# Linear attention with a row norm and a gated feed-forward on one core: the start, the place of batch 2's loads, the norm chains, the query tails and the last tile are changed

## The chip, the core and the metric

The kernel runs on one core of a Trainium2 chip. The metric is device microseconds of one execution, as the median of three runs. A profile is one further execution of the same program, recorded by the hardware profiler. The core's engines are TensorE (PE, with weight loads shown as PEld), VectorE (DVE), ScalarE (ACT), GpSimd (POOL) and SyncE (SP), which here only issues DMAs. Each engine works through its own instructions in program order.

## The reference

For 8 batches and 8 heads, with 576 rows and 64 columns a head, without softmax:

```
kv  = k^T v                      per batch and head, 64 x 64
o   = q kv                       576 x 64
a   = o / sqrt(mean(o*o) + 1e-6) * g_norm          over the 64 columns
x   = a, heads side by side      4608 rows x 512
xn  = x / sqrt(mean(x*x) + 1e-6) * rms_g           over the 512 columns
g, val = xn @ w_gate, xn @ w_val                   512 x 1536 each
out = (g * sigmoid(g) * val) @ w_out               1536 x 512, result 4608 x 512 fp32
```

All inputs are fp32; the kernel rounds them to bf16 for the products.

## The kernel before

**Tiles.** Of each batch 512 rows are "main" (four tiles of 128, `T` = 4) and 64 are "tail". The tails of all eight batches are gathered into a ninth block, so that the feed-forward runs nine times over 512 rows: n = 0 to 7 for the batches, n = 8 for the tails. `Ffn.up(j)` makes 128 columns of gate and value (8 matmuls of 512 columns), `silu` on ACT, the product `h` on DVE; there are 12 of them. `Ffn.down(c)` multiplies `h` with w_out for one tile of 128 rows (12 matmuls), four times, and `down_out` copies the sum on ACT and stores it from SP.

**The order.** It is written out by hand; nothing is moved by a planner. While block n is in the feed-forward, the attention of n+1 is put between its steps by the lists `steps[u]` (u = 0 to 11 stand behind `up(u)`, 12 to 15 behind `down(u - 12)`): kv products, `o(c)` (PE, then a square and a copy on ACT), `sums(c)` (DVE), and at step 11 `chain` (DVE: both norms' factor alpha, with an inverse root by a bit trick and two Newton steps), `scale(c)` (DVE) and `x_rows(c)` (SP: a DMA transpose of a scaled tile into `xnt`, which the next block's `up(0)` reads).

**PSUM.** Four pools of two banks each: `gps` and `vps` for gate and value, `ops` for the output, `att` for attention. `up(j)` can start only when `silu` of `up(j-2)` has read its `gps` bank.

**Loads.** All loads but a few at the start go through SP, in program order, into the `stage` pool of seven buffers of 1 MB: batch 0, then the weights (`load_w`, four blocks), batch 1 and w_out (three blocks). Batch 2 is loaded in line 685, near the end of block 0, behind block 0's first store. `load_batch(n + 2)` at the start of block n does it for batch 3 and on. ACT casts batch 2's q in `steps[0]` and `steps[1]` of block 1, and `q_rows` (SP, DMA transposes, behind the loads of batch 3 on SP's queue) turns it for `o(0)` at step 6. For blocks 2 and on these casts and transposes are done one block earlier, behind the downs.

**Batch 0 and 1** use `Early`: the sums of squares are made on PE from a transposed output, `Early.chain` works on them in PSUM, and x is turned on PE (`turn`). For batch 0 this is the start of the kernel, with parts of `up` of 128 and 256 columns as soon as a tile of x is there. The sources are `first_kv`, `gammas`, lines 468 to 607.

**Query tails.** At the start of block 6 `load_q_tails` issues eight loads of 128 KB from SP; ACT casts them behind the downs of block 6 (`cast_q_tails`, two casts, one for the even and one for the odd batches) and SP turns them (`turn_q_tails`, eight DMA transposes) for the ninth block's `o(0)`, which stands at step 2 of block 7.

Of the kernel before, what the change touches and what calls it, by code (L numbers as in the profile page):

```python
# [1 line left out]

# [15 lines left out]
def kernel(  # L18
# [61 lines left out]
    mask = consts.tile([128, 128], FP32, name="mask")  # L80
    sqT = consts.tile([128, NS, MAIN], BF16, name="sqT")
# [95 lines left out]
    def chain(u, w, nc_, name):  # L177
# [10 lines left out]
        )  # L188
        yi = stat_pool.tile(shape, I32, name=name + "yi")
# [20 lines left out]
    class Att:  # L210
# [103 lines left out]
    class Ffn:  # L314
# [29 lines left out]
        def down_out(self, c):  # L344
            if c % 2 == 0:
                self.o_sb = osb_pool.tile([128, 2, d_model], FP32, name="o_sb")
            nc.scalar.copy(out=self.o_sb[:, c % 2, :], in_=self.o_ps[c])  # L347
            n = self.n
# [10 lines left out]
        def down(self, c):  # L359
            self.down_products(c, 0, NF)  # L360
# [21 lines left out]
    nc.scalar.preload_act_table(ACT.Silu)  # L382
# [11 lines left out]
    nc.vector.memset(warm_sb, 0.0)  # L394
    nc.vector.memset(sel, 0.0)
# [5 lines left out]
    nc.vector.memset(ones1, 1.0)  # L401
    nc.vector.memset(kv_all[:, 1:], 0.0)

    def warm(ps, count, w=256):
        for _ in range(count):
            nc.tensor.matmul(ps[:, 0:w], lhsT=identity, rhs=warm_sb[:, 0:w], start=True, stop=True)  # L406
# [4 lines left out]
    class Early:  # L411
# [62 lines left out]
    for half, engine in enumerate((nc.vector, nc.scalar)):  # L474
        ps = ops_pool.tile([128, 2, T, 128], BF16, name="o_ps")
        for j in range(2):
            for c in range(T):
# [4 lines left out]
                )  # L482
        cast(engine, first.qt[:, 2 * half : 2 * half + 2, :], ps.rearrange("p j c t -> p j (c t)"))
        if half == 0:
            cast_tail(0, "k", nc.vector)
            cast_tail(0, "v", nc.scalar)
            cast_piece(0, "k", 0, nc.vector)
            cast_piece(0, "v", 0, nc.scalar)
            cast_piece(0, "k", 1, nc.vector)

# [3 lines left out]

    def gammas():
        nc.vector.tensor_copy(out=gcol, in_=gam_ps[:, NS : NS + 1])
        nc.vector.tensor_scalar(
            out=rowscale, in0=gam_ps[:, 0:NS], scalar1=gcol[:, 0:1], scalar2=None, op0=OP.mult
        )
        for i in range(2):  # L500
            ps_ = slice(i * D, (i + 1) * D)
            nc.vector.scalar_tensor_tensor(
                out=sel[ps_, 1, i : i + 1], in0=gcol[ps_, :], scalar=1.0 / d_model, in1=gcol[ps_, :],
                op0=OP.mult, op1=OP.mult,
            )
# [4 lines left out]
    def first_kv(j):  # L510
        hs = slice(2 * j, 2 * j + 2)
        ps = att_pool.tile([128, 128], FP32, name="att_ps")
        warm(ps, 3, 128)
# [5 lines left out]

    cast_piece(0, "v", 1, nc.scalar)  # L520
    first_kv(0)
    gammas()
    first_kv(1)
    sq_ps = [first.out_turned(0, gps_pool, "g_ps")]
    first.square(0, sq_ps[0])
    cast_piece(0, "k", 2, nc.vector)
    cast_piece(0, "v", 2, nc.scalar)
    sq_ps.append(first.out_turned(1, gps_pool, "g_ps"))
    first.square(1, sq_ps[1])
    first_kv(2)  # L530
    cast_piece(0, "k", 3, nc.vector)
    cast_piece(0, "v", 3, nc.scalar)
    sq_ps.append(first.out_turned(2, vps_pool, "v_ps"))
    first.square(2, sq_ps[2])
    first_kv(3)
    first.square(3, first.out_turned(3, vps_pool, "v_ps"))
    first.sums(0, gps_pool, "g_ps")
    first.sums(1)
    first.sums(2)
    first.o(0, ops_pool, "o_ps")  # L540
    first.o(1, ops_pool, "o_ps")
    first.sums(3)
    first.chain()
# [9 lines left out]
    warm(vps_pool.tile([128, MAIN], FP32, name="v_ps"), 16)  # L553


# [29 lines left out]
    for c in range(3):  # L585
        first.scale(c)
        if c < 2:
            first.turn((c,), ops_pool, "o_ps", nc.scalar)
        if c == 0:
            p = Up(ffn, 0, 0, 128)  # L590
            p.products()
            p.silu()
    p.h()
    p = Up(ffn, 1, 0, 128)
    p.products()
    p.silu()
    first.turn((2,), att_pool, "att_ps", nc.scalar)
    first.scale(3)
    p.h()
    p = Up(ffn, 0, 128, 256)  # L600
    p.products()
    p.silu()
    first.turn((3,), att_pool, "att_ps", nc.scalar)
    p.h()
# [9 lines left out]
    for blk in range(3):  # L614
        load_wo(blk)

    gsq_ps = att_pool.tile([128, D], FP32, name="att_ps")
    nc.vector.scalar_tensor_tensor(
        out=gsq1, in0=gn1, scalar=1.0 / d_model, in1=gn1, op0=OP.mult, op1=OP.mult
    )  # L620
    nc.tensor.matmul(gsq_ps, lhsT=ones1, rhs=gsq1, start=True, stop=True)
    nc.vector.tensor_copy(out=gsq8[:, 0, :], in_=gsq_ps)
    for n in (1, 2, 4):
        nc.vector.tensor_copy(out=gsq8[:, n : 2 * n, :], in_=gsq8[:, 0:n, :])
# [14 lines left out]
    for j in range(4, NF):  # L639
        ffn.up(j)  # L640
        for name, s in extras.get(j, ()):
            round_w(3, name, s, nc.scalar if name == "g" else nc.vector)
        for name, i in casts.get(j, ()):
# [12 lines left out]
    att.q_turn(0, nc.scalar)  # L656
    att.q_turn(1, nc.vector)
# [5 lines left out]
    for j in range(NS):  # L663
        second.square(j, second.out_turned(j, att_pool, "att_ps"))
# [20 lines left out]
    load_batch(2)  # L685
# [38 lines left out]
    for n in range(1, B + 1):  # L724
# [7 lines left out]
        if n == 1:  # L732
# [19 lines left out]
            steps[11].append(nxt.chain)  # L752
            for c in range(T):
                steps[11] += [lambda c=c: nxt.scale(c), lambda c=c: nxt.x_rows(c)]
        elif nxt is not None:
# [6 lines left out]
            steps[11].append(nxt.chain)  # L762
# [61 lines left out]
```

## Time and profile before

| | us |
|---|---|
| median of three runs (lowest, highest) | 355.76 (354.92, 356.06) |
| the profiled execution, whole | 355.0 |
| its span, first to last instruction | 353.2 |
| TensorE busy in it (weight loads apart) | 319.8 (91%) |
| VectorE, ScalarE busy in it | 180.9 (51%), 183.9 (52%) |
| blocks 2 to 6, each from its first matmul to the next block's | 33.6 to 34.0 |
| block 1 | 44.9 |
| block 7 | 37.7 |
| before block 1 | 66.0 |
| block 8 to the end | 35.9 |

The profile gives time from the first instruction. Rows of the timeline merge like instructions that follow each other: start, length, engine, line, operation, written tile, read tiles, count, and in brackets how long the engine idled before it and what ended that idling. The mean granted TensorE clock of the execution is 0.984 of full speed.

### The profile page before, as it was taken

The numbers are of one execution on the slowest core, as the hardware profiler recorded it, in microseconds if no ns is written. First come the engines' busy times: TensorE is split into PE (matmuls) and PEld (weight loads), VectorE is DVE, ScalarE is ACT, GpSimd is POOL, SyncE is SP. The second block draws the span as 40 slices with busy tenths as digits, with TensorE's granted clock in tenths as the row PEclk, the third lists the DMA queues.
The fourth block names the chain that finished last, engine by engine and source line by source line (L and its number), as shares of the span: only waits on it lengthen the run. The fifth ranks groups of instructions, "written<-read, shape, count | busy, mean of one in ns | idle before, by whom it ended". The sixth has DMA issues, their size and how long they took to land.

```text
span 353.2 us, 4868 instructions
## 1 busy us (share of the span) xinstructions
PE 319.8 (91%) x1782; PEld 158.1 (45%) x1782; DVE 180.9 (51%) x398; ACT 183.9 (52%) x333; POOL 19.4 (5%) x36
## 2 busy tenths in 40 slices
PE   2688999909998999999999999999999969999994
PEld 1365454504444544444444445444544435444441
DVE  4366774305691587167626742773478217733410
ACT  3537574326757556655666385539464535323321
POOL 6050130000000000000000040000000000000000
PEclk9999999978999999999999999999999989999999
DMA  8999950999206881696269329934720641032014
GB/s 227 349 380 347 347 196 12 294 331 269 47 8 155 216 248 25 154 299 150 44 177 306 100 59 181 302 86 119 181 57 0 149 92 59 0 97 84 0 32 90
DMA packets 79256, 55.38 MB, mean 157 GB/s; under 512 B 46460, under 2 KB 73088, under 8 KB 79232
## 3 DMA queue, kind: packets, MB, share of 16 engines
q1 hardware_dynamic: 77248, 53.62, 55.3%
q10 hardware_dynamic: 1856, 1.44, 1.4%
q8 instruction: 14, 0.23, 0.3%
q14 instruction: 10, 0.08, 0.1%
q0 software_dynamic: 128, 0.00, 0.0%
HBM read 37.75 MB, written 9.44 MB: 134 GB/s over the span
## 4 chain that ended last, share of the span: by engine, by line
PE 65%; DVE 13%; DMA 11%; SPq 6%; ACT 2%; issue 2%; DVEq 0%; ACTq 0%
PE g_ps L327 24%; PE v_ps L327 23%; PE o_ps L339 9%; DVE xna L289 4%; SPq L296 4%; DMA xnt<-xna 3%; DMA st<-in_k_dram 3%; DMA st<-in_q_dram 3%; DVE h_sb L333 2%; PE att_ps L264 2%; PE att_ps L225 2%; DMA qt<-qb 2%; SPq L722 1%; PE v_ps L406 1%; DMA st<-st 1%
## 5 line engine op out<-in xcount | busy, mean ns | idle before, releaser
L333 DVE TENSOR_TENSOR h_sb<-silu,v_ps 128x512 bf16<-128x512 bf16 (+2 forms) x109 | 73.6, 676 | 131.6 <-PE v_ps L327 120.9
L327 PE MATMUL g_ps<-xnt,wg_sb 128*128 128x512 bf16 (+2 forms) x436 | 112.1, 380 | 12.3 <-ACT silu L332 8.0
L327 PE MATMUL v_ps<-xnt,wv_sb 128*128 128x512 bf16 (+2 forms) x436 | 111.4, 378 | 0.0
L332 ACT ACTIVATE silu<-g_ps 128x512 bf16<-128x512 f32 (+2 forms) x109 | 64.7, 594 | 70.2 <-PE g_ps L327 70.2
L339 PE MATMUL o_ps<-wo_sb,h_sb 128*128 128x512 bf16 x432 | 95.4, 379 | 0.1
L327 PEld LDWEIGHTS <-wv_sb 128*128 128x128 bf16 x436 | 42.9, 99 | 51.2 <-issue 1.9
L327 PEld LDWEIGHTS <-wg_sb 128*128 128x128 bf16 x436 | 40.6, 99 | 55.4 <-issue 15.7
L339 PEld LDWEIGHTS <-h_sb 128*128 128x128 bf16 x432 | 42.1, 98 | 50.8 <-issue 0.8
L347 ACT COPY o_sb<-o_ps 128x512 f32<-128x512 f32 x36 | 21.1, 586 | 43.8 <-PE o_ps L339 43.7
L269 ACT ACTIVATE sq<-att_ps 128x512 bf16<-128x512 f32 x28 | 16.7, 597 | 17.9 <-PE att_ps L264 17.5
L99 ACT CAST qb<-st 128x512 bf16<-128x512 f32 (+1 forms) x25 | 14.2, 636 | 11.7 <-DMA st<-in_q_dram 11.7
L99 ACT CAST vb<-st 128x512 bf16<-128x512 f32 x32 | 18.4, 618 | 2.3 <-DMA st<-in_v_dram 2.3
L279 DVE TENSOR_REDUCE ssq<-sq 128x8 f32<-128x512 bf16 x28 | 19.0, 678 | 0.0
L280 DVE TENSOR_REDUCE wssq<-wsq 128x8 f32<-128x512 bf16 x28 | 18.9, 675 | 0.0
L289 DVE TENSOR_TENSOR xna<-outa,sy 128x512 bf16<-128x512 bf16 x28 | 17.5, 686 | 0.2
L271 ACT CAST outa<-att_ps 128x512 bf16<-128x512 f32 x28 | 16.2, 579 | 0.0
L715 POOL MEMSET st<- 64x2048 bf16 x2 | 3.6, 1800 | 156.2 <-ACT qb L99 155.4
L278 DVE TENSOR_TENSOR wsq<-sq,gsq 128x512 bf16<-128x512 bf16 x28 | 11.7, 418 | 0.0
L99 ACT CAST kb<-st 128x512 bf16<-128x512 f32 x20 | 10.9, 618 | 0.0
L225 PEld LDWEIGHTS <-kb 128*128 128x128 bf16 x140 | 8.9, 98 | 3.3 <-issue 0.2
L225 PE MATMUL att_ps<-vb,kb 128*128 128x128 bf16 x140 | 10.1, 219 | 0.1
L264 PEld LDWEIGHTS <-qt 128*128 128x128 bf16 x96 | 7.3, 98 | 6.2 <-DMA qt<-qb 0.8
(111 smaller groups left out, 160.4 us busy)
## 6 DMA issues: line engine op xcount, KB each, us to landing
out_dram<-o_sb SPq DMA_DIRECT2D x16, 512.0 KB, 3.3
st<-in_k_dram SPq DMA_DIRECT2D x7, 1024.0 KB, 10.5
st<-in_v_dram SPq DMA_DIRECT2D x7, 1024.0 KB, 10.9
st<-in_q_dram SPq DMA_DIRECT2D x7, 1024.0 KB, 7.5
st<-in_moe_w_out_dram SPq DMA_DIRECT2D x3, 1024.0 KB, 10.4
st<-in_moe_w_gate_dram SPq DMA_DIRECT2D x2, 1024.0 KB, 11.6
st<-in_moe_w_val_dram SPq DMA_DIRECT2D x2, 1024.0 KB, 13.4
rawt<-in_k_dram SPq DMA_DIRECT2D x8, 128.0 KB, 10.0
```

The lines of the kernel that those rows point to most:

```text
L99: engine.copy(out=dst, in_=src)
L225: nc.tensor.matmul(self.kv_ps[:, j, :], lhsT=bufs[n]["k"][:, c, hs, :], rhs=bufs[n]["v"][:, c, hs, :], start=(j == 0 and c == 0), stop=(j ...
L269: nc.scalar.activation(out=self.sq, in_=ps, func=ACT.Square)
L271: nc.scalar.copy(out=self.outa[c], in_=ps)
L279: nc.vector.reduce_sum(out=self.ssq[:, c, :], in_=self.sq, axis=AX.X)
L280: nc.vector.reduce_sum(out=self.wssq[:, c, :], in_=wsq, axis=AX.X)
L289: nc.vector.tensor_tensor(out=self.xna[c], in0=self.outa[c], in1=self.alpha[:, c, :].to_broadcast([128, H, D]), op=OP.mult)
L327: nc.tensor.matmul(ps[:, 0:w], lhsT=wt[:, s, j * 128 : (j + 1) * 128], rhs=x[:, s, lo:hi], start=(s == 0), stop=(s == NS - 1),)
L332: nc.scalar.activation(out=silu[:, 0:w], in_=g_ps[:, 0:w], func=ACT.Silu)
L333: nc.vector.tensor_tensor(out=self.h[:, j, lo:hi], in0=silu[:, 0:w], in1=v_ps[:, 0:w], op=OP.mult)
L339: nc.tensor.matmul(self.o_ps[c], lhsT=self.h[:, j, c * 128 : (c + 1) * 128], rhs=wo_sb[:, j, :], start=(j == 0), stop=(j == NF - 1),)
L347: nc.scalar.copy(out=self.o_sb[:, c % 2, :], in_=self.o_ps[c])
```

## The change

It does seven things.

1. PE runs 24 dummy products from the start and 18 more behind the gammas; the dummies in `first_kv` change in number. The gammas and `gsq1` are made ahead of the casts of k and v; the tail casts and one cast of v move (`cast_piece(0, "v", 2)` to POOL); the weights' block 0 is rounded on POOL alone.
2. `Early.sums` begins with two products that put eps into the sums, so that `Early.chain` loses its add.
3. Batch 0's chain becomes `chain_by_scalar`: five DVE operations and four `Sqrt` on ACT. The activation table preloaded at the start is Sqrt's, and Silu's is loaded behind the four roots.
4. `load_wo` and `load_batch(2)` stand directly behind `load_batch(1)` on SP. The product that spreads `g_norm` moves from behind `up(3)` to behind `up(6)`. `q_turn` and two of the `out_turned` of batch 1 use other PSUM pools.
5. `chain` is split: `mean` at step 10, `root` at step 11.
6. In block 6 the casts of the query tails move from behind the downs to steps 3 and 4, their transposes to steps 5 to 10.
7. The last output tile is made in two column halves in two PSUM banks, copied by DVE and ACT, and stored from SP and ACT.

```diff
-    nc.scalar.preload_act_table(ACT.Silu)
+    nc.scalar.preload_act_table(ACT.Sqrt)
...
+    warm(gps_pool.tile([128, MAIN], FP32, name="g_ps"), 24)
...
         def sums(self, j, pool_=None, name=None):
             if j == 0:
                 self.st = pool_.tile([128, T, 2, H], FP32, name=name)
+                for i in range(2):
+                    nc.tensor.matmul(self.st, lhsT=ones1, rhs=eps_row[:, i], start=(i == 0), stop=False)
...
+        def chain_by_scalar(self):
+            r = stat_pool.tile([128, T, H], FP32, name="sr")
+            nc.vector.reciprocal(out=r, in_=self.st[:, :, 0, :])
+            nc.vector.tensor_tensor(out=terms[:, :, 0:H], in0=r, in1=self.st[:, :, 1, :], op=OP.mult)
+            m = stat_pool.tile([128, T], FP32, name="sm")
+            nc.vector.reduce_sum(out=m, in_=terms, axis=AX.X)
+            rm = stat_pool.tile([128, T], FP32, name="rm")
+            nc.vector.reciprocal(out=rm, in_=m)
+            self.alpha = stat_pool.tile([128, T, H], FP32, name="sy1")
+            for c in range(T):
+                nc.scalar.activation(
+                    out=self.alpha[:, c, :], in_=r[:, c, :], func=ACT.Sqrt, scale=rm[:, c : c + 1]
+                )
...
+    warm(gps_pool.tile([128, MAIN], FP32, name="g_ps"), 18)
...
+    cast_piece(0, "v", 2, nc.gpsimd)
...
+    first.chain_by_scalar()
+    nc.scalar.preload_act_table(ACT.Silu)
...
-    for s in range(NS):
-        round_w(0, "g", s, nc.scalar)
-    for s in range(NS):
-        round_w(0, "v", s, nc.gpsimd)
-    for name in "gv":
-        for s in range(NS):
-            round_w(1, name, s, nc.gpsimd)
+    for blk in range(2):
+        for name in "gv":
+            for s in range(NS):
+                round_w(blk, name, s, nc.gpsimd)
...
     load_batch(1, "kvq")
+    for blk in range(3):
+        load_wo(blk)
+    load_batch(2)
...
-    for blk in range(3):
-        load_wo(blk)
...
-    att.q_turn(0, nc.scalar)
-    att.q_turn(1, nc.vector)
+    att.q_turn(0, nc.scalar, gps_pool, "g_ps")
+    att.q_turn(1, nc.vector, gps_pool, "g_ps")
...
-        second.square(j, second.out_turned(j, att_pool, "att_ps"))
+        where = (att_pool, "att_ps") if j < 2 else (vps_pool, "v_ps")
+        second.square(j, second.out_turned(j, *where))
...
-    load_batch(2)
     ffn.down_products(3, 0, NF)
...
-            steps[11].append(nxt.chain)
+        if nxt is not None:
+            steps[10].append(nxt.mean)
+            steps[11].append(nxt.root)
             for c in range(T):
                 steps[11] += [lambda c=c: nxt.scale(c), lambda c=c: nxt.x_rows(c)]
...
         if n == B - 2:
             for u in range(2):
-                steps[NF + u].append(lambda u=u: cast_q_tails(u, nc.scalar))
+                steps[3 + u].append(lambda u=u: cast_q_tails(u, nc.scalar))
                 for c in range(T):
-                    steps[NF + 2].append(lambda u=u, c=c: turn_q_tails(u, c))
+                    steps[(5, 5, 6, 7, 8, 8, 9, 10)[4 * u + c]].append(lambda u=u, c=c: turn_q_tails(u, c))
...
+            if n == B and c == T - 1:
+                for i in range(2):
+                    cols = slice(256 * i, 256 * i + 256)
+                    ps = self.o_halves[i]
+                    cast((nc.vector, nc.scalar)[i], self.o_sb[:, 1, cols], ps[:, cols])
+                    for u in range(2):
+                        r0 = (2 * c + u) * S + MAIN
+                        (nc.sync, nc.scalar)[u].dma_start(
+                            out=out[r0 : r0 + TAIL, cols], in_=self.o_sb[u * TAIL : (u + 1) * TAIL, 1, cols]
+                        )
+                return
```

## Rows read from the trace of the kernel before

**Rows 1.** Waits: engine, line, releaser: total us, times, longest.
```profile
PE g_ps L327 <- DMA xnt<-xna: 3.7, 6, 1.3
```

**Rows 2.** Timeline of the start, batch 0.
```profile
3.24 1.28 ACT L382 ACT_TABLE_LOAD   x1 [3.24 <-issue]
...
20.35 0.19 DVE L446 TENSOR_SCALAR u<-g_ps 128x32 f32<-128x32 f32 x1 [1.96 <-PE g_ps L431]
...
20.98 3.57 PE L406 MATMUL v_ps<-warm_sb,identity 128*128 128x256 bf16 x16
...
23.63 1.29 DVE L451 TENSOR_TENSOR xna<-o_ps,sy 128x512 bf16<-128x512 f32 x2
...
25.45 0.38 PE L567 MATMUL g_ps<-xnt,wg_sb 128*128 128x128 bf16 x4 [0.67 <-ACT xnt L99]
```

**Rows 3.** Timeline, end of block 0 and the first product of block 1.
```profile
42.57 2.67 POOL L101 CAST qb<-st 128x512 bf16<-128x512 f32 x4 [20.14 <-DMA st<-in_q_dram]
...
47.91 1.04 POOL L101 CAST wo_sb<-st 128x1024 bf16<-128x1024 f32 x1 [2.67 <-DMA st<-in_moe_w_out_dram]
...
55.18 1.89 PE L339 MATMUL o_ps<-wo_sb,h_sb 128*128 128x512 bf16 x8
...
66.00 1.03 PE L327 MATMUL g_ps<-xnt,wg_sb 128*128 128x512 bf16 x4
```

**Rows 4.** Timeline of block 1: up(3), q's transposes, o(0); in block 2 the loads' start.
```profile
79.32 1.86 PE L327 MATMUL g_ps<-xnt,wg_sb 128*128 128x512 bf16 x4 [7.98 <-ACT silu L332]
...
83.65 6.33 SPq L238 DMA_TRANSPOSE qt<-qb  x4
...
89.54 0.40 PE L264 MATMUL att_ps<-kv_all,qt 128*128 128x128 bf16 x4 [0.27 <-DMA qt<-qb]
...
117.29 0.39 SPq L116 DMA_DIRECT2D st<-in_q_dram  x1
```

**Rows 5.** Windows of block 1: us, busy of PE to POOL, PEclk, DMA share, GB/s.
```profile
76.00:79.30 3.30, 0.00 (x0) 0.00 (x0) 0.00 (x1) 1.67 (x4) 0.00 (x0) 0.50 1.08 337
79.30:82.60 3.30, 3.28 (x9) 1.21 (x9) 2.37 (x5) 3.30 (x7) 0.00 (x0) 0.53 1.12 337
```

**Rows 6.** Source L108, block 2's last tail load: start and landing.
```profile
L108 SPq DMA_DIRECT2D rawt<-in_v_dram x1: 2699/2699/2699, 123.4 to 123.4; - x1
...
DMA to landing us min/median/max: 8.7/8.7/8.7
```

**Rows 7.** Timeline, first products of blocks 6, 7, 8; DVE at block 6's last up.
```profile
245.91 1.04 PE L327 MATMUL g_ps<-xnt,wg_sb 128*128 128x512 bf16 x4 [0.35 <-DMA xnt<-xna]
...
268.92 0.69 DVE L333 TENSOR_TENSOR h_sb<-silu,v_ps 128x512 bf16<-128x512 bf16 x1 [0.65 <-PE v_ps L327]
269.52 0.18 DVE L284 TENSOR_SCALAR u<-ssq 128x32 f32<-128x32 f32 x1
...
270.79 0.18 DVE L190 TENSOR_SCALAR syi<-sz 128x32 int32<-128x32 int32 x1
...
279.61 1.02 PE L327 MATMUL g_ps<-xnt,wg_sb 128*128 128x512 bf16 x4 [0.43 <-DMA xnt<-xna]
...
317.26 1.04 PE L327 MATMUL g_ps<-xnt,wg_sb 128*128 128x512 bf16 x4 [0.38 <-DMA xnt<-xna]
```

**Rows 8.** Source L708, the seventh of eight tail loads in block 6.
```profile
L708 SPq DMA_DIRECT2D st<-in_q_dram x1: 633/633/633, 255.5 to 255.5; - x1
...
DMA to landing us min/median/max: 4.5/4.5/4.5
```

**Rows 9.** Timeline: up(6) of block 6, the tail cast, block 7's o(0), the last copy.
```profile
257.85 1.03 PE L327 MATMUL g_ps<-xnt,wg_sb 128*128 128x512 bf16 x4
...
271.92 1.90 ACT L99 CAST st<-st 64x2048 bf16<-64x2048 f32 x1
...
287.66 0.93 PE L264 MATMUL att_ps<-kv_all,st 128*128 128x128 bf16 x7 [2.65 <-DMA st<-st]
...
348.55 0.59 ACT L347 COPY o_sb<-o_ps 128x512 f32<-128x512 f32 x1 [2.00 <-PE o_ps L339]
```

More of the change, by code (lines that the diff above doesn't have):

```diff
@@ L359, in down @@
         def down(self, c):
-            self.down_products(c, 0, NF)
+            if self.n == B and c == T - 1:
+                self.o_halves = [
+                    pool_.tile([128, d_model], FP32, name=name)
+                    for pool_, name in ((gps_pool, "g_ps"), (vps_pool, "v_ps"))
+                ]
+                for i in range(2):
+                    for j in range(NF):
+                        nc.tensor.matmul(
+                            self.o_halves[i][:, 256 * i : 256 * i + 256],
+                            lhsT=self.h[:, j, c * 128 : (c + 1) * 128], rhs=wo_sb[:, j, 256 * i : 256 * i + 256],
+                            start=(j == 0), stop=(j == NF - 1),
+                        )
+            else:
+                self.down_products(c, 0, NF)
             self.down_out(c)
@@ L394, with warm @@
     nc.vector.memset(warm_sb, 0.0)
+    def warm(ps, count, w=256):
+        for _ in range(count):
+            nc.tensor.matmul(ps[:, 0:w], lhsT=warm_sb[:, 0:128], rhs=warm_sb[:, 0:w], start=True, stop=True)
+    warm(gps_pool.tile([128, MAIN], FP32, name="g_ps"), 24)
     nc.vector.memset(sel, 0.0)
@@ L429, in sums @@
                 self.st = pool_.tile([128, T, 2, H], FP32, name=name)
+                for i in range(2):
+                    nc.tensor.matmul(self.st, lhsT=ones1, rhs=eps_row[:, i], start=(i == 0), stop=False)
             for c in range(T):
@@ L482, with first_kv @@
                 )
+        if half == 1:
+            cast_tail(0, "v", nc.scalar)
         cast(engine, first.qt[:, 2 * half : 2 * half + 2, :], ps.rearrange("p j c t -> p j (c t)"))
[L484 to L489, printed above, removed]
+    cast_tail(0, "k", nc.vector)
     gam_ps = att_pool.tile([128, 8], FP32, name="att_ps")
     nc.tensor.matmul(gam_ps[:, 0:5], lhsT=gam[0:5, :], rhs=ident32[0:5, 0:5], is_transpose=True, start=True, stop=True)
[L495 to L498, printed above, removed]
[L499 to L505 removed]
+    warm(gps_pool.tile([128, MAIN], FP32, name="g_ps"), 18)
+    nc.vector.tensor_copy(out=gcol, in_=gam_ps[:, NS : NS + 1])
+    nc.vector.tensor_scalar(
+        out=rowscale, in0=gam_ps[:, 0:NS], scalar1=gcol[:, 0:1], scalar2=None, op0=OP.mult
+    )
+    for i in range(2):
+        ps_ = slice(i * D, (i + 1) * D)
+        nc.vector.scalar_tensor_tensor(
+            out=sel[ps_, 1, i : i + 1], in0=gcol[ps_, :], scalar=1.0 / d_model, in1=gcol[ps_, :],
+            op0=OP.mult, op1=OP.mult,
+        )
+    nc.vector.scalar_tensor_tensor(
+        out=gsq1, in0=gn1, scalar=1.0 / d_model, in1=gn1, op0=OP.mult, op1=OP.mult
+    )
     alloc_xnt(0)
[L510 removed]
+    def first_kv(j, dummies):
         hs = slice(2 * j, 2 * j + 2)
         ps = att_pool.tile([128, 128], FP32, name="att_ps")
[L513 removed]
+        warm(ps, dummies, 128)
         for c in range(T + 1):
@@ L584, with part @@
     load_batch(1, "kvq")
[L585 to L596, printed above, removed]
+    for blk in range(3):
+        load_wo(blk)
+    load_batch(2)
+    def part(j, lo, hi):
+        p = Up(ffn, j, lo, hi)
+        p.products()
+        p.silu()
+        return p
+    first.scale(0)
+    first.scale(1)
+    first.turn((0,), ops_pool, "o_ps", nc.vector)
+    first.turn((1,), ops_pool, "o_ps", nc.scalar)
+    p0 = part(0, 0, 128)
+    first.scale(2)
+    p1 = part(1, 0, 128)
     first.turn((2,), att_pool, "att_ps", nc.scalar)
+    p0.h()
     first.scale(3)
[L599 to L602, printed above, removed]
+    p1.h()
+    p0 = part(0, 128, 256)
     first.turn((3,), att_pool, "att_ps", nc.scalar)
-    p.h()
+    p0.h()
     ffn.up(1, 128, 256)
@@ L642 @@
             round_w(3, name, s, nc.scalar if name == "g" else nc.vector)
+        if j == 6:
+            gsq_ps = att_pool.tile([128, D], FP32, name="att_ps")
+            nc.tensor.matmul(gsq_ps, lhsT=ones1, rhs=gsq1, start=True, stop=True)
+            nc.vector.tensor_copy(out=gsq8[:, 0, :], in_=gsq_ps)
+            for n in (1, 2, 4):
+                nc.vector.tensor_copy(out=gsq8[:, n : 2 * n, :], in_=gsq8[:, 0:n, :])
         for name, i in casts.get(j, ()):
```

79 lines of the change are left out of this document (39 added, 40 removed).

## The prediction

> **What bounds the kernel now.** I read the stage lengths first (the table above), then the waits, then the timeline around each stage that is longer than its fellows. TensorE is busy for 91% of the span, so only its idle places and its slow stretches can be won. There are five. (1) Before block 1: 66.0 us. Block 0 cannot end before w_out is there: its second block is cast on POOL as it lands, at 47.91 [rows 3]. (2) Block 1 has one stall: up(3) starts at 79.32, 7.98 us late, since ACT sits in the cast of batch 2's q, and the clock is at the lower level (0.50) when it resumes [rows 4, 5]. (3) At each later block's start PE waits for the DMA transposes of x: 3.7 us in six places [rows 1]. (4) Block 7 waits 2.65 us for the query tails' transposes [rows 9]. (5) The last copy and store follow the last product [rows 9]. Everything else on DVE and ACT runs beside PE.
>
> **The change, part by part**, summed against the profiled execution (355.0 us; median 355.76, so it lies low among the runs by 0.8).
>
> *Start (parts 1 to 4).* The 12 DVE steps of batch 0's chain take 23.63 - 20.35 = 3.28 us [rows 2]. Four that stay, at that mean of 0.27, and one root on ACT (about 0.3, as one step) make 1.4: 1.9 us saved. The DVE add is replaced by two products; at 0.2 us each (the 16 dummies of 256 columns take 3.57 us, so 0.22 each, which is 1.2 GHz [rows 2]) they stand on PE before the last squares and cost nothing. That row also says that PE is slow as late as 24 us: with the dummies in front I expect 2.4 GHz in the whole prologue, and between the landing of v and the chain there are some 50 products of 0.1 to 0.6 us in series with casts. With one cast of v taken from ACT and the gammas ahead I put 3.5 us on this, between 0.5 (only the cast) and 4. The dummies themselves lie before data has landed; were the clock still low they would delay the first kv products by about 1.5 us. Silu's table load (1.28 [rows 2]) stands behind the roots, beside two scales on DVE (1.29 [rows 2]): at most 0.3 on the path. The weights' block 0 goes to POOL, 4 more roundings of the size of its others, done some 1 us before the first up needs them. Spreading g_norm behind up(6) costs DVE about 0.9 us in a stage where it has slack.
>
> So x of batch 0 comes 5 us or more earlier. How much of it reaches block 1 the loads decide. Batch 1's q lands at 42.57 and its POOL casts end at 45.24; w_out's second block lands at 47.91 and is cast by 48.95 [rows 3]. SP's order up to there is unchanged and the DMA engines have no pause, so I leave these times. From the products that need that cast (55.18) to block 1's first (66.00) are 10.82 us [rows 3]: block 1 starts at 48.95 + 10.82 = 59.8, **6.2 us earlier**. Bounds: 3.0 if only the chain's 1.9 and the moved g_norm product come through, 6.5 if all waits vanish. The compute has about 1.7 us to spare (it would stand waiting for q's casts), so this term hangs on the loads.
>
> A rule: the Trainium skill (ScalarE: Activation LUTs, What ACT_TABLE_LOAD costs) gives a change of table set 1283 ns for the load, as the row has it, and about 1380 ns more to drain; my estimate from it is 1.4 us more on the path. By the row the start keeps 1.7 us to spare, by the page 0.3; that bears on rival C alone.
>
> *Batch 2's loads (part 4).* They follow w_out at once, into buffers that are free by then, and should land at about 59, since 3.4 MB (three of 1.05, two of 0.13) take some 10 us at the 337 GB/s of rows 5. ACT's cast of q is due at about 61, so the stall goes. The 7.98 us of idling go [rows 4], and the slow stretch (3.3 us at half clock [rows 5]) gives 1.6 back: 9.6.
>
> What is late next: q's transposes. On SP they stand behind the loads of batch 3, which go out after block 0's last store. Let S be block 1's start. o(0) was at 89.54 - 66.00 = 23.5 after it [rows 4]; without stall S + 13.6 (9.6 less, and 0.3 of its own wait). The loads of batch 3 start at S + 1.4 (last copy 0.8, store's issue 0.6). In block 2 the same five loads go from 117.29 [rows 4] to 123.4 + 8.7 = 132.1 [rows 6]: 14.8 us. The transposes issued at 83.65 landed when o(0) could start, 5.9 us later [rows 4], as the loads ahead of them drained. So the first lands at about S + 1.4 + 14.8 + 0.5 = S + 16.7: a new wait of 3.0 us at o(0), between 0 and 4. A wait of that length in block 7 (2.65 [rows 9]) was followed by slow products; I add 1.1 for the clock. Behind the waiting o(0) stand up(7) and all of PE. Block 1 is thus shorter by 9.6 + 0.3 - 3.0 - 1.1 = **5.8 us**.
>
> *Two-part chain (part 5).* DVE idles 0.65 us before the last h; `mean` is 270.79 - 269.52 = 1.27 us long [rows 7]. Put before that h it fills the gap and delays h by 0.6, which down(0) needs only as its twelfth factor. So x comes 0.65 earlier, and the waits of 0.35 to 0.43 [rows 7] plus the drained pipeline (0.1) vanish. The largest wait, 1.3 [rows 1], belongs to block 1, where DVE has no gap: no gain there. Six others at (3.7 - 1.3) / 5 = 0.48: **2.9 us**. Bounds 0 and 3.5.
>
> *Query tails (part 6).* Gone is block 7's wait: it lasts 317.26 - 279.61 = 37.65, block 6 279.61 - 245.91 = 33.70 [rows 7]; with 1.1 of kv products less and 0.9 of tail products more it should take 33.5, so **4.2 us** are won. But the casts now stand on ACT between silu(3) and silu(4) of block 6. The seventh load, the last of the even half, is issued at 255.54 and lands 4.5 us later, at 260.05 [rows 8]; nothing ahead of it on SP moves against block 6's start. ACT waits for it from about 254.2 (an up is eight products of 512 columns, 1.71 us at 2.4 GHz; up(6) starts at 257.85 [rows 9], so up(4) some 3.6 before it, and silu(3) ends there), casts for 1.90 [rows 9], and only then comes silu(4), at 262.0 to 262.6. up(6) needs that bank: it starts at 262.65 instead of 257.85 [rows 9], 4.8 us idle. Behind it ACT has o(1)'s two copies (1.2), the second cast (1.9) and silu(5), so up(7) starts at 266.3 to 266.5 instead of 259.8 (257.85, an up and a tile of o). **6.6 us lost**, whether the clock falls in between or not, since the second wait hides a slow up(6). Bounds: 0 (the loads are there) and 8.
>
> *Last tile (part 7).* The copy is half as wide (0.59 [rows 9], so about 0.4) and one store's issue of some 0.5 is beside the other's: **0.6 us**, between 0 and 1.
>
> Sum: 355.0 - 6.2 - 5.8 - 2.9 + 6.6 - 4.2 - 0.6 = 341.9; with a little for the low profile, **342.0 us**.
>
> **The rivals.**
> A. The tail cast does not wait, because the tails land sooner beside a quieter queue. For: they wait only for SP's turn. Against: 260.05 lies 5.8 us behind ACT's need. Time 342.0 - 6.6 = 335.4.
> B. q's transposes do not wait behind batch 3's loads. Then 4.1 less: 337.9. Against it stands the 5.9 us of rows 4; for it stands that SP issues them from about S + 10 on (117.29 to the end of the last issue, 123.4 + 2.7, is 8.8 [rows 4, 6]), 3 us ahead of the need.
> The Trainium skill says so too (DMA: Bandwidth & Descriptors, Two DMAs through the same engine are not ordered): descriptors of one queue start in order, but a later transfer may complete before an earlier one. The trace's transposes kept behind the loads.
> C. The start gives 3 us: compute, not loads, sets block 1's start. 342.0 + 3.2 = 345.2. For: that half of the 5 us on batch 0 is estimated.
> D. Slower. The clock falls in block 6's idle 4.8 us and does not rise while PE goes on in pieces, waiting for ACT. From up(7) to block 7 are 279.6 - 259.8 = 19.8 us of work, at half clock twice as long: 342.0 + 19.8 = 362. It decides from about 15 us of such work on. Against: in block 1 full speed was back at 82.6, 3.3 us after the products resumed [rows 5].
> E. Batch 2's loads are early in issue only: a buffer still in use holds SP, q lands some 3 us after ACT asks for it, and block 1 keeps that wait beside the other: 342.0 + 3.0 + 1.1 = 346.1. For: they take the buffers that batch 1's k and v leave. Against: those are cast ahead of batch 1's q, and its casts end at 45.24 [rows 3].
>
> **How the numbers follow.** Forecast 0.49 (its own range 339.5 to 344), A 0.13, B 0.15, C 0.10, E 0.05, D 0.05, and 0.03 that nothing of it holds and no change is left. Range 335 to 347: it takes in A, B, C and E. A measurement of this kernel tells 0.3% (1.1 us) from nothing. Faster (forecast, A, B, C, E) 0.92, same 0.03, slower (D) 0.05.
>
> **What would show it.** Block 1's first product at about 59.8, right behind w_out; no wait of silu there, but o(0) idle some 3 us for q's transposes; blocks 2 to 5 about 33.2 long, with no wait for x; in block 6 the cast of the tails waiting about 6 us for a load, and up(6) and up(7) late by 6.6 together; block 7 at 33.5. Wrong it would be if block 6 runs like block 5, or if block 1 starts after 62.

## The result, and the profile after

The changed kernel takes 344.81 us (median of three runs, 344.48 to 344.82) against 355.76: ratio 0.9694, 95% interval 0.9667 to 0.9721. That is faster, inside the range, by 2.8 us less than forecast. The profiled execution is of 344.82 us, its span 343.0 (353.2 before), TensorE busy for 93% of it.

Lengths from one block's first up product to the next one's (the last row: to the end), in us, read from the timelines. The four kernels to the right are experiments that are told below.

| | before | forecast | after | tails back | tails on GpSimd | queries first | both |
|---|---|---|---|---|---|---|---|
| start to block 1 | 66.0 | 59.8 | 61.43 | 61.39 | 61.26 | 61.13 | 61.46 |
| block 1 | 44.93 | 39.1 | 41.78 | 41.50 | 41.83 | 34.76 | 34.75 |
| blocks 2 to 5, each | 34.04 to 33.60 | 33.2 | 33.09 | 33.09 | 33.09 | 33.09 | 33.09 |
| block 6 | 33.70 | 39.8 | 39.55 | 33.09 | 33.09 | 39.44 | 33.33 |
| block 7 | 37.65 | 33.0 | 32.87 | 35.43 | 32.87 | 32.87 | 32.86 |
| block 8 to the end | 35.9 | 35.3 | 35.01 | 35.02 | 35.00 | 35.01 | 35.00 |

The waits of TensorE in the changed kernel over the whole span (engine, written tile, line, releaser: total us, times, longest):

```profile
PE att_ps L272 <- DMA qt<-qb: 5.0, 1, 5.0
PE g_ps L338 <- ACT silu L343: 4.5, 1, 4.5
...
PE o_ps L350 <- ACT wo_sb L103: 0.5, 1, 0.5
PE o_ps L350 <- POOL wo_sb L105: 0.5, 1, 0.5
PE g_ps L338 <- DMA xnt<-xna: 0.5, 1, 0.5
```

The six waits for x of [rows 1] are down to one, of 0.5 us, at block 2's start. Two waits stand out: for transposed queries in block 1 (line 272 is `o`; 0.27 us before [rows 4]), and for a silu in block 6, where there was none.

**The start**, from the timelines of VectorE, ScalarE and TensorE (start, length, engine, line, operation, tiles, count, idle time before):

```profile
18.40 0.36 DVE L494 RECIPROCAL sr<-g_ps 128x32 f32<-128x32 f32 x1 [1.43 <-PE g_ps L476]
...
19.78 1.29 DVE L508 TENSOR_TENSOR xna<-o_ps,sy 128x512 bf16<-128x512 f32 x2 [0.37 <-ACT sy L502]
```
```profile
19.45 0.87 ACT L502 ACTIVATE sy<-sr,rm 128x8 f32<-128x8 f32 x4 [1.40 <-DVE rm L499]
20.34 1.28 ACT L600 ACT_TABLE_LOAD   x1
21.63 0.59 ACT L103 COPY xnt<-o_ps 128x512 bf16<-128x512 bf16 x1
```
```profile
21.45 0.38 PE L622 MATMUL g_ps<-xnt,wg_sb 128*128 128x128 bf16 x4
```

From the sums to the first scaling it is 1.38 us (3.28 before [rows 2]), and the first up product comes 4.0 us earlier. The end of block 0 is held elsewhere, by w_out's second block:

```profile
48.73 1.56 POOL L105 CAST wo_sb<-st 128x1024 bf16<-128x1024 f32 x1 [3.13 <-DMA st<-in_moe_w_out_dram]
```
```profile
48.70 0.69 DVE L105 CAST wo_sb<-st 128x1024 bf16<-128x1024 f32 x1 [1.29 <-DMA st<-in_moe_w_out_dram]
```
```profile
50.34 1.89 PE L350 MATMUL o_ps<-wo_sb,h_sb 128*128 128x512 bf16 x8 [0.51 <-POOL wo_sb L105]
...
61.43 0.81 PE L338 MATMUL g_ps<-xnt,wg_sb 128*128 128x512 bf16 x3
```

The cast that started at 47.91 and took 1.04 [rows 3] starts at 48.73 and takes 1.56, beside a cast by VectorE that starts 0.03 us ahead of it.

**Block 1**: SyncE's queue, TensorE's timeline, and two windows (us; busy time of PE, PEld, DVE, ACT, POOL; granted clock, 1.00 being 2.4 GHz; DMA share; GB/s):

```profile
62.65 0.43 SPq L120 DMA_DIRECT2D st<-in_q_dram  x1
...
68.11 3.88 SPq L112 DMA_DIRECT2D rawt<-in_v_dram  x1
72.09 8.20 SPq L246 DMA_TRANSPOSE qt<-qb  x4
```
```profile
80.06 0.61 PE L272 MATMUL att_ps<-kv_all,qt 128*128 128x128 bf16 x4 [5.00 <-DMA qt<-qb]
80.46 1.91 PE L338 MATMUL g_ps<-xnt,wg_sb 128*128 128x512 bf16 x4
```
```profile
75.20:80.00 4.80, 0.00 (x0) 0.00 (x0) 0.65 (x1) 0.00 (x0) 0.00 (x0) 0.72 1.50 156
80.00:84.20 4.20, 4.14 (x16) 1.91 (x17) 0.02 (x1) 1.67 (x3) 0.00 (x0) 0.50 0.26 50
```

The silu's stall of [rows 4] is gone. The queries' transposes stand behind batch 3's loads on SyncE; o(0) waits 5.0 us for the first of them, and TensorE comes out of the wait at half clock.

**Block 6**, ScalarE and TensorE:

```profile
249.73 1.90 ACT L103 CAST st<-st 64x2048 bf16<-64x2048 f32 x1 [5.86 <-DMA st<-in_q_dram]
251.53 0.59 ACT L343 ACTIVATE silu<-g_ps 128x512 bf16<-128x512 f32 x1
```
```profile
252.17 1.87 PE L338 MATMUL g_ps<-xnt,wg_sb 128*128 128x512 bf16 x4 [4.51 <-ACT silu L343]
```

ScalarE waits 5.86 us for a tail load, casts, and only then runs silu(4), for whose bank up(6) waits 4.51 us.

### The profile page after: what moved, and what is told of

Its sections match the earlier page's. It is cut to its first block, busy times and chain, and to the rows that moved or that the text cites. A ratio compares the mean times of both kernels' runs of the same rounds, so it can differ in the third digit from the quotient of the medians.

```text
span 343.0 us, 4934 instructions
## 1 busy us (share of the span) xinstructions
PE 319.7 (93%) x1795; PEld 161.0 (47%) x1828; DVE 177.5 (52%) x395; ACT 182.9 (53%) x332; POOL 21.4 (6%) x41
## 4 chain that ended last, share of the span: by engine, by line
PE 71%; DMA 9%; DVE 7%; ACT 4%; SPq 4%; issue 3%; POOL 1%; ACTq 0%; DVEq 0%; POOLq 0%
PE g_ps L338 22%; PE v_ps L338 22%; PE o_ps L350 20%; DMA st<-in_moe_w_out_dram 3%; DMA qt<-qb 2%; DVE h_sb L344 2%; DMA gam<-in_g_norm_dram 2%; PE att_ps L272 2%; SPq L762 2%; SPq L246 2%; PE att_ps L233 1%; PE g_ps L433 1%; DMA st<-in_q_dram 1%; DVE ssq L287 1%; ACT kb L103 1%
## 5 line engine op out<-in xcount | busy, mean ns | idle before, releaser
L338 PE MATMUL g_ps<-xnt,wg_sb 128*128 128x512 bf16 (+2 forms) x419 | 109.9, 380 | 6.1 <-ACT silu L343 4.5
L350 PE MATMUL o_ps<-wo_sb,h_sb 128*128 128x512 bf16 x410 | 92.2, 379 | 2.0 <-ACT wo_sb L103 0.5
L350 PEld LDWEIGHTS <-h_sb 128*128 128x128 bf16 x420 | 40.9, 98 | 50.9 <-issue 1.4
L277 ACT ACTIVATE sq<-att_ps 128x512 bf16<-128x512 f32 x28 | 16.7, 597 | 20.0 <-PE att_ps L272 19.6
L103 ACT CAST vb<-st 128x512 bf16<-128x512 f32 x31 | 17.7, 618 | 1.6 <-DMA st<-in_v_dram 1.6
L272 PE MATMUL att_ps<-kv_all,qt 128*128 128x128 bf16 x96 | 9.6, 225 | 5.0 <-DMA qt<-qb 5.0
```

Of the source, the lines that this page charges most:

```text
L103: engine.copy(out=dst, in_=src)
L272: nc.tensor.matmul(ps[:, 2 * j : 2 * j + 2, :], lhsT=a, rhs=b, start=(j == 0 and i == 0), stop=(j == NS - 1 and i == len(terms) - 1),)
L277: nc.scalar.activation(out=self.sq, in_=ps, func=ACT.Square)
L338: nc.tensor.matmul(ps[:, 0:w], lhsT=wt[:, s, j * 128 : (j + 1) * 128], rhs=x[:, s, lo:hi], start=(s == 0), stop=(s == NS - 1),)
L350: nc.tensor.matmul(self.o_ps[c], lhsT=self.h[:, j, c * 128 : (c + 1) * 128], rhs=wo_sb[:, j, :], start=(j == 0), stop=(j == NF - 1),)
```

## The experiments

The theory after the result: two waits made by the change itself, in blocks 1 and 6, hold back some 13 us; what else the change wins stands. Each experiment edits the changed kernel, and its profile is read by block.

**1. The tails as before** (`e1_tails_back`).

```
- steps[3 + u].append(lambda u=u: cast_q_tails(u, nc.scalar))
+ steps[NF + u].append(lambda u=u: cast_q_tails(u, nc.scalar))
- steps[(5, 5, 6, 7, 8, 8, 9, 10)[4 * u + c]].append(...turn_q_tails(u, c))
+ steps[NF + 2].append(...turn_q_tails(u, c))
```

> The changed kernel with only the query tails as before: both tail casts go back to ScalarE after block 6's first two down tiles, and the turns behind them. Theory: of the changed kernel's block 6 (39.55 us against 33.1 for blocks 2 to 5) the 6.4 us above its neighbours are ScalarE's wait for the tails' landing (5.86 us ahead of the first tail cast) and its consequences; without it block 6 is 33.1 to 33.7 us and block 7 pays its old 4.2 to 4.8 us again for turns that come late: total 344.8 - 6.2 + 4.5 = 343.1 us. Rival: block 6 is long for another reason (the tail loads' traffic on the DMA rings): then block 6 stays near 39 and the total goes up to 349.

Measured: 341.23 us, ratio 0.9601 (0.9553 to 0.9648). Block 6 falls to 33.09, so its 6.46 us over the neighbours were the cast's place and not the loads' traffic. Block 7 grows by 2.56 only, not 4.5, and its timeline and windows say why:

```profile
276.13 0.56 PE L272 MATMUL att_ps<-kv_all,st 128*128 128x128 bf16 x7 [2.39 <-DMA st<-st]
```
```profile
273.50:276.00 2.50, 0.24 (x2) 0.00 (x0) 0.69 (x1) 0.00 (x0) 0.00 (x0) 1.00 0.52 105
276.00:280.00 4.00, 3.82 (x23) 1.99 (x25) 1.48 (x3) 2.17 (x4) 0.00 (x0) 1.00 0.53 113
```

The wait is 2.39 us long and the granted clock stays at 1.00. Before, the wait was 2.65 [rows 9], and the same windows of the kernel before show the fall:

```profile
285.00:287.60 2.60, 0.00 (x1) 0.00 (x0) 0.69 (x1) 0.00 (x0) 0.00 (x0) 0.92 0.51 104
287.60:291.00 3.40, 3.34 (x15) 1.73 (x16) 0.00 (x0) 1.67 (x3) 0.00 (x0) 0.56 0.46 82
```

Taken alone, the move of the tails loses 3.9 us, by the lengths of these two blocks.

**2. The tail casts on GpSimd** (`e2_tails_pool`).

```
- steps[3 + u].append(lambda u=u: cast_q_tails(u, nc.scalar))
+ steps[3 + u].append(lambda u=u: cast_q_tails(u, nc.gpsimd))
```

> The changed kernel with only the engine of the two tail casts changed, GpSimd for ScalarE, at the same places. GpSimd's casts of 128x1024 took 1.30 us, so a 64x2048 tail should take about 2.6 us there and delay nobody. Theory (a cast that waits for its load holds the silus queued behind it): ScalarE never waits, block 6 falls from 39.55 to 33.1 us and block 7 stays at 32.9: total 338.4 us. Rival 1: the tail loads themselves slow block 6, whoever casts them: 344 to 345. Rival 2: GpSimd is slower or the turns come too late for block 7, which then grows by 1 to 4 us: 339.5 to 342.5.

Measured: 339.03 us, 0.9538 (0.9504 to 0.9571). Block 6 is 33.09 and block 7 32.87; TensorE has no wait at all in the two.

```profile
249.19 3.83 POOL L105 CAST st<-st 64x2048 bf16<-64x2048 f32 x2 [47.30 <-DMA st<-in_q_dram]
```

GpSimd waits for the same load, and nobody is queued behind it. It does each cast in 1.9 us, as ScalarE does, and not in the 2.6 expected: the 1.30 that I started from is the mean of a free cast (1.04) and the one of 1.56 shown above. The early turn was good; the engine that had to wait for it was the mistake.

**3. Queries ahead of the loads** (`e3_q_first`).

```
  if 1 < n + 2 < B:          ->   if 3 < n + 2 < B:
  steps[1] (block 1), behind the four q_rows:
+ steps[1].append(lambda: load_batch(3, "qkv"))
```

> The changed kernel with only batch 3's loads issued behind the four transposes of batch 2's queries instead of ahead of them (both on SyncE, in block 1). Theory: the transposes were late (issued at 72.09, first landed at 80.01, o(0) due at 75.1) because the SyncE queue held batch 3's loads ahead of them; with the loads behind, o(0) runs when it is due, block 1 loses the wait of 5.0 us and the 2.1 us that the low clock after it cost: block 1 from 41.78 to about 34.7, total 337.7. Rival 1: the transposes wait for data of the stores or of batch 2's casts anyway: no change, 344.8. Rival 2: the wait goes, but batch 3's loads then come too late for their casts at the end of block 1: part of the 7 us is given back in block 2, total 339 to 343.

Measured: 337.41 us, 0.9495 (0.9461 to 0.9529); block 1 34.76, as the theory said to 0.1. SyncE's queue, o(0), and the window in which TensorE had idled:

```profile
65.67 5.22 SPq L246 DMA_TRANSPOSE qt<-qb  x4
70.93 0.59 SPq L120 DMA_DIRECT2D st<-in_q_dram  x1
```
```profile
74.59 0.39 PE L272 MATMUL att_ps<-kv_all,qt 128*128 128x128 bf16 x4
```
```profile
75.20:80.00 4.80, 4.75 (x28) 2.41 (x28) 3.54 (x8) 4.05 (x9) 0.00 (x0) 1.00 1.04 302
```

Batch 3's loads go out 8.3 us later, and block 2 pays nothing for it.

**4. The wait filled** (`e4_hold_clock`).

```
+ steps[6].append(lambda: warm(att_pool.tile([128, 256], FP32, name="att_ps"), 44))
```

> The changed kernel with 44 products of 128x128 by 128x256 on zeros put into TensorE's queue just ahead of o(0) in block 1, where it waits 5.0 us for the transposed queries: they fill the wait (44 by about 0.11 us at full clock) and move nothing else. Theory: the granted clock of 0.72 and 0.50 from 75.2 to 84.2 us comes of the wait, and costs about 2.1 us after it: with the wait filled the clock stays full and the total falls by 2.1 us to 342.7. Rival 1: what comes after the wait is limited by ScalarE and VectorE, not by the clock: no change, 344.8. Rival 2: the products run longer than the wait and push o(0) later: up to 346.

Measured: block 1 goes from 41.78 to 39.71, the 2.1 us expected:

```profile
75.20:80.00 4.80, 4.80 (x45) 4.14 (x43) 0.69 (x1) 0.00 (x0) 0.00 (x0) 1.00 1.31 158
80.00:84.20 4.20, 4.14 (x28) 2.19 (x29) 1.86 (x4) 3.15 (x6) 0.00 (x0) 1.00 0.27 54
```

The whole time does not show it: 344.03, ratio 0.968 (0.9642 to 0.9719), which overlaps the changed kernel's. In the profiled execution one later block was 0.68 us longer by a late transpose of x, and block 6 0.65 longer. So the 7.0 us of experiment 3 are 5.0 of wait and 2.1 of clock.

**5. Without the start's dummies** (`e5_no_warm`).

```
- warm(gps_pool.tile([128, MAIN], FP32, name="g_ps"), 24)
- warm(gps_pool.tile([128, MAIN], FP32, name="g_ps"), 18)
```

> The changed kernel without the 24 dummy products at its start and the 18 behind the gains (the few among the key-value products stay). Theory: the start's end is held by the output weights of block 1 (landed 48.67, cast, then 11.09 us of work), and between the first up product (21.45) and block 1 (61.43) TensorE waits only 1.3 us in all, so a later first product is hidden up to 1.3 us and counts beyond. Without the dummies the key-value products, transposes and sums before the roots run at half clock; they take some 5 us at full clock, half of it hidden beside VectorE and ScalarE: first up product about 2.5 us later (24.0), block 1 some 1.2 us later, total 346.0. Rival 1: the weights alone hold it: 344.8. Rival 2: the clock is the whole of the early gain: first up product at 25.5, block 1 3 us later, 347.6. Rival 3: the first key-value product comes 0.9 us earlier without the 18 in front of it, and nothing is lost: 344.

Measured: 343.34 us, 0.9628 (0.9594 to 0.9662); first up product 21.90, block 1 at 61.58. The theory is wrong: here the dummies are worth 0.45 us of the first product and 0.15 of block 1's start, as rivals 1 and 3 had it. That is hardly more than scatter: ten kernels with the changed kernel's start have their first up product between 20.86 and 21.76 and block 1 between 61.13 and 61.71. The slower products are partly paid by an earlier start, since the 18 dummies of the changed kernel run at half clock and push the first key-value products from 11.78 to 12.79:

```profile
9.20:12.80 3.60, 3.60 (x20) 2.56 (x21) 1.58 (x7) 1.28 (x3) 0.20 (x1) 0.54 1.09 348
```

The total is even lower, by 1.13 us in block 1 (the queries' wait is 3.0 there, not 5.0) and 0.69 in block 6. Both ride on when loads land; why they landed sooner stays open. The nine kernels that leave block 6's casts on ScalarE have that block between 38.86 and 40.46.

**6. Batch 0's roots on VectorE** (`e6_dve_chain0`).

```
- nc.scalar.preload_act_table(ACT.Sqrt)
+ nc.scalar.preload_act_table(ACT.Silu)
- first.chain_by_scalar()
- nc.scalar.preload_act_table(ACT.Silu)
+ first.chain()
```

> The changed kernel with batch 0's roots by VectorE's integer chain again, in place of four Sqrt activations on ScalarE, and the Silu table loaded at the start (so the table load of 1.28 us at 20.34 goes too). Theory: from the reciprocal to the first scaling it was 3.28 us before and 1.38 now: the first up product comes 1.9 us later (23.35), of which 1.3 us are hidden by TensorE's waits up to block 1: block 1 starts 0.6 us later, total 345.4. Rival 1: all of it shows: 346.7. Rival 2: the output weights hold block 1's start in any case: 344.8.

Measured: 346.18 us, 0.9713 (0.968 to 0.9746), which overlaps the changed kernel's; the blocks tell more. The first up product comes at 23.61, 2.16 us later, and block 1 2.28 us later, at 63.71: nothing of it is hidden, though TensorE had waits of 1.3 us to give. The chain takes 3.68 us (18.25 to 21.93), not 3.28. TensorE waits 3.12 us for it, and behind that wait the granted clock is 0.50 from 24.5 to 27.8 us (four products of 128 columns take 0.63 us there in place of 0.39). Then w_out's casts, now due together, take more:

```profile
48.83 1.04 POOL L105 CAST wo_sb<-st 128x1024 bf16<-128x1024 f32 x1 [3.14 <-DMA st<-in_moe_w_out_dram]
```
```profile
48.90 1.52 DVE L105 CAST wo_sb<-st 128x1024 bf16<-128x1024 f32 x1
```

Here GpSimd starts first and keeps its 1.04, and VectorE's cast takes 1.52 in place of 0.69. Block 1 is shorter by 1.39, again in its wait for queries (4.0).

**7 and 11. Batch 2's loads later** (`e7_load2_back`, `e11_load2_exact`). In 7 `load_batch(2)` stands at the head of block 1's loop. I called that the old place, and it is not: before, it stood ahead of block 0's last down tile and last store. Run 11 has it there.

```
- load_batch(2)                        # behind load_wo, both runs
+ load_batch(2)                        # run 7: head of the loop, n == 1
+ load_batch(2)                        # run 11: ahead of ffn.down_products(3, 0, NF)
```

> The changed kernel with batch 2's loads issued at the head of block 1, as before, instead of right behind the output weights. Theory: this step is what removes the key-value wait of block 1; its cost comes back: block 1 from 41.78 to about 45 us, total 348. Block 1's start stays at 61.4, since these loads stand behind the weights in the queue. Rival 1: block 1's start comes earlier without 3 MB of other loads on the rings: up to 0.5 us of it returned. Rival 2: with the later loads batch 3's come later too and the queries wait still longer: block 1 at 47 to 49, total 350 to 352.

> The changed kernel with batch 2's loads at the very place of the kernel before: after the turns of block 1's x and ahead of the last down tile of block 0, before the last store of that block. There they should be issued some 57.7 us in (61.19 before, whose block 1 began at 66.00). Theory: the loads' age at block 1's start is what the stall hangs on: before, queries landed 16.4 us after the first issue; here they would land at about 74.1, 12.7 us behind block 1's start at 61.4 (11.6 before), so the first silu waits 8 to 9 us as before, block 1 is 45 to 46 us and the total 348 to 349. Rival: the loads can't start before SyncE's queue is free of the first store, and are as late as one step further on: block 1 near 51, total 354.

Measured: 354.62 us, 0.9939 (0.9911 to 0.9968), block 1 50.93; and 350.06, 0.9861 (0.9805 to 0.9917), block 1 46.64. ScalarE's first cast of queries in 7, then in 11:

```profile
78.11 1.14 ACT L103 CAST qb<-st 128x512 bf16<-128x512 f32 x2 [15.03 <-DMA st<-in_q_dram]
```
```profile
73.27 1.14 ACT L103 CAST qb<-st 128x512 bf16<-128x512 f32 x2 [10.22 <-DMA st<-in_q_dram]
```

The silu behind it holds TensorE for 13.0 and 8.2 us. So at its old place the loads' step costs 4.9 us of block 1, net of the queries' wait (1.0 in place of 5.0). One step further on, block 2 begins at 112.35, later than before the change (110.93): the earlier start of block 1 is gone whole, because ScalarE asks sooner for queries that land no sooner.

**8. The chain in one piece** (`e8_one_part`).

```
- steps[10].append(nxt.mean)
- steps[11].append(nxt.root)
+ steps[11] += [nxt.mean, nxt.root]
```

> The changed kernel with the root chain in one piece again, all of it behind up unit 11 (the five instructions of the mean moved back from behind unit 10). Theory: blocks 2 to 5 go from 33.09 to about 33.6 us, blocks 1, 6 and 7 get 0.5 us each as well, since the transposes to the next block's first product come 0.5 us later: 7 by 0.5, total 348.3. Rival 1: the gap is the transposes' landing and not VectorE's chain: blocks stay at 33.1, total 344.8. Rival 2: only blocks 2 to 5 and 7 show it (block 1 and 6 end on other waits): 347.3.

Measured: 348.65 us, 0.9775 (0.9749 to 0.98), above the changed kernel. Blocks 2 to 5 are 33.61 to 33.77 long, 2.44 more in all, and block 7 is longer by 0.48; block 1 is not (41.65). Block 6 is longer by 0.91 (40.46), but it reaches 40.35 in experiment 7, which leaves it as it was; so its share is not told. The row of [rows 1] is back:

```profile
PE g_ps L338 <- DMA xnt<-xna: 3.3, 6, 1.2
```

**12. The last tile in one piece** (`e12_last_tile_back`).

```
- if n == B and c == T - 1:            # in down_out and in down
+ if False:
```

> The changed kernel with the last output tile in one piece, as before (one product chain of 512 columns, one copy by ScalarE, two stores). Theory: the halves let the first copy and its stores run beside the second half's products, so that what lies behind the last product is a half copy instead of a whole one: 0.9 us come back in block 8 (35.01 to 35.94), total 345.7. Rival: the 0.9 us come of the chain in two parts (block 8 opens with a wait for its x before, and with none after): then block 8 stays within 0.3 of 35.0 and the total at 344.8 to 345.1.

Measured: 345.45 us, 0.9731 (0.9681 to 0.978), which cannot be told from 0.9694; but block 8 is 35.94 long in place of 35.01, by a copy of 0.59 in place of one of 0.37, and by what follows it. The copies after the last product, in this run and in the changed kernel:

```profile
338.86 0.59 ACT L370 COPY o_sb<-o_ps 128x512 f32<-128x512 f32 x1 [2.00 <-PE o_ps L350]
```
```profile
339.30 0.37 ACT L103 COPY o_sb<-v_ps 128x256 f32<-128x256 f32 x1 [2.03 <-PE v_ps L389]
339.70 0.50 ACTq L366 DMA_DIRECT2D out_dram<-o_sb  x1
```

**9 and 10. Both waits taken away, and the dummies too** (`e9_both`: edits 2 and 3; `e10_both_no_warm`: edits 2, 3 and 5).

> The changed kernel with both waits taken away: the query tails' casts on GpSimd, and batch 3's loads behind the transposes of batch 2's queries. Theory: the two waits lie in blocks 1 and 6 and have nothing in common, so their gains add: block 1 at 34.76 as with the second alone, block 6 at 33.09 as with the first alone, total 337.4 - 6.4 = 331.0. Rival: one gives back part of the other (batch 3's later loads, or GpSimd's casts beside a fuller VectorE): 332 to 335.

> The kernel with both waits taken away, and without the 24 and 18 dummy products of the start. With the dummies gone from the changed kernel alone, the first up product came 0.45 us later and block 1 0.15 us later, but block 1 itself was 1.1 us shorter, by its wait for the queries, which is gone here. Theory (the dummies of the start buy nothing that reaches the end): within 0.5 us of the kernel with them, 331.0 to 331.5. Rival: they are worth their first 0.45 us and the clock through the start: 331.5 to 333.

Measured: 332.04 us, 0.9356 (0.9299 to 0.9413), and 332.61, 0.937 (0.9323 to 0.9417). The gains add to within 1 us, and this version beats both kernels. Its longest waits of TensorE behind the first transposes of batch 0:

```profile
PE o_ps L516 <- DVE xna L508: 1.0, 2, 0.8
PE g_ps L257 <- POOL qb L105: 0.7, 2, 0.3
PE g_ps L338 <- DMA xnt<-xna: 0.5, 1, 0.5
```

Without the dummies the first up product comes at 23.10 in place of 20.86 here, yet block 1 only 0.38 later: much of the rest lies in TensorE's waits for GpSimd's casts of q (0.7) and of w_out (0.5), which are gone without the dummies. The two totals cannot be told apart. The first up product in experiment 5, and here:

```profile
21.90 0.38 PE L620 MATMUL g_ps<-xnt,wg_sb 128*128 128x128 bf16 x4
```
```profile
23.10 0.59 PE L620 MATMUL g_ps<-xnt,wg_sb 128*128 128x128 bf16 x4
```

The same products take 0.38 us in one run and 0.59 in the other.

## Why the prediction was right, and where its sizes were off

The forecast case came, each mechanism at the place it was put. Its sizes were off: 344.81 lies above the forecast's own range (339.5 to 344), and only the wider range, drawn to take in the rivals, holds it. Of the sum, two terms were too good by 4.3 us, and four others together too poor by 1.4.

**Start (-6.2; measured -4.57).** That w_out sets block 1's start held, but "I leave these times" did not: the cast started 0.82 us later and took 0.52 more, and the products behind it 0.27 more; 1.6 in all. The 0.82 is not settled. Landings run late from 5.7 us on, SyncE's loads wait for stage buffers, and the delay grows: the second block of weights goes out 0.20 us later, batch 1's queries 0.44, w_out 0.79 (35.55, 34.76 before). Batch 2's loads are not the cause (without them there, in experiments 7 and 11, the cast starts at 48.72 and 48.70), nor are the dummies or the roots (48.88 and 48.83 in 5 and 6). The 0.52 is GpSimd beside VectorE. The Trainium skill (SBUF — State Buffer, Who interferes with whom) says that VectorE in its modes with two ports, which casts can enter, and GpSimd share a pair of ports, and that whoever issues first has it for a whole instruction while the other is blocked. The traces agree both ways round: VectorE 0.03 us ahead, GpSimd 1.56 for 1.04 (the same in eleven kernels); GpSimd 0.07 ahead (experiment 6), VectorE 1.52 for 0.69. Both are 0.14 us shorter than if the second cast had stood still until the first one's end.

The share given to the clock was too large: I put 3.5 us on a prologue at 2.4 GHz. Without the dummies the first product came 0.45 us later in one pair of kernels and 2.2 in the other, and block 1 0.15 and 0.38. The clock itself tells the two apart. The trace's records of the granted clock begin with 1.00 at 5.66 us in the changed kernel, at 15.93 in experiment 5, at 24.14 in experiment 10 and at 24.37 before the change, and products ahead of that are slow (0.59 us for 0.38 above). So the dummies do bring full speed forward, but little of it reaches block 1. It did not last through the prologue either: in the changed kernel the clock was 0.50 from 9.07 to 12.48. The rest of the 4.0 us, from the casts and gammas that moved and from a new order of the first scalings and turns (which the list of changes leaves out), was not run alone.

The roots on ScalarE are worth 2.3 us at block 1's start, more than the 1.9 that I took; the fall of the clock and the slow cast of experiment 6 are in this. Rival C put block 1 at 63.0, held by compute; 61.43 lies halfway. On the way there TensorE waits for casts of what was loaded (0.33 us for q, 0.51 for w_out), so compute alone does not set the start. How much compute has to spare (1.7 us in the prediction) is not settled: a first product 2.24 us later moved block 1 by 0.38 in experiment 10, one 2.16 later by 2.28 in experiment 6. That the total lies next to C's 345.2 is chance: 2.65 us of the gap to the forecast come from block 1, of which C says nothing. The drain that the Trainium skill (ScalarE: Activation LUTs, What ACT_TABLE_LOAD costs) adds to a table load does not show in this trace: the load starts 0.02 us after the last root, and the next copy 0.01 after the load.

**Block 1 (-5.8; measured -3.15): the step that failed.** The stall went, as said; the wait put in its place was mis-sized. The landing at S + 16.7 took 14.8 us for batch 3's loads from block 2, where just one store, which lands within 3.5 us, is issued right ahead of them. Here the last of them, issued at 68.11, landed 11.4 later, at 79.5, 16.9 after the first issue at 62.65:

```profile
L112 SPq DMA_DIRECT2D rawt<-in_v_dram x1: 3879/3879/3879, 68.1 to 68.1; - x1
...
DMA to landing us min/median/max: 11.4/11.4/11.4
```

When they began, more was on the way: batch 2's queries landed at 63.5 and block 0's two stores at 64.8 and 66.3. That these took the 2.1 us is read from the trace and not tested. So o(0) waited 5.0 us, not 3.0, and the clock took 2.1, not 1.1 (experiments 3 and 4). Rival B did not come: a transpose took up to 7.9 us from issue to landing behind the loads, 2.5 to 4.0 ahead of them. Rival E is out: ScalarE waited 0.42 us for q.

**Two-part chain (-2.9).** Measured 2.62 in blocks 2 to 5 alone; experiment 8 gives back 2.44 there and 0.48 in block 7, none of it in block 1, as said. Whether block 6 adds to this (0.91 in experiment 8) and the upper bound of 3.5 was too low, its scatter does not tell. The sum counts six waits of 0.48 where [rows 1] has five beside the largest; the block without one fell as far as the others.

**Tails (+6.6 and -4.2).** Block 6 lost 6.46. The gain of block 7 was right against the kernel before, but only 2.56 of it come back in experiment 1; the other 1.6 are the wait's last quarter of a microsecond and the slow products behind it, which the shorter wait does not have. Rival A is out: ScalarE waited 5.86. Rival D is out: 4.51 us of idling, slow products until 255, then full speed.

**Last tile (-0.6).** Measured -0.93.

## What to carry to other kernels

A step that waits for a transfer belongs on an engine with nothing urgent behind it: the same casts at the same places cost 6.5 us on ScalarE and nothing on GpSimd. When work is moved ahead, read the issuing queue for what now stands in front of the small transfer that is needed first; here four transposes behind five loads cost 7 us. And a wait has two prices, its length and the clock after it, which only the windows tell apart.

## What was not expected of the hardware

- A wait of 2.39 us left the granted clock at 1.00, one of 2.65 dropped it to about half for the 3.4 us behind it, and one of 5.00 for 4.2 us. One case each.
- VectorE's small steps are slower beside GpSimd's roundings: in experiment 6's chain the same step of 128x32 (line 204) took 0.42 us at 19.82, while GpSimd rounded weights, and 0.19 at 21.16, in GpSimd's only pause (0.29 us, for a load).
- The first 24 dummies of 256 columns took 5.03 us, 0.21 each (the 44 of experiment 4 took 4.97, so 0.11), while the windows print a granted clock of 1.00 for that stretch. The trace has no record of the clock before 5.66 us, and the windows print 1.00 where there is none. For the 18 that follow at the same pace there is one, 0.50 (0.54 over their whole window).
